# Gated linear attention and a GELU FFN on one core: casts and copies of the second unit on other engines, and a new order

## The chip, the cores and the metric

The kernel runs on one core of a Trainium2 chip. TensorE (PE) multiplies matrices, VectorE (DVE), ScalarE (ACT) and GpSimd (POOL) do the elementwise work, SyncE (SP) issues most of the transfers, and 16 DMA engines carry them. The metric is the time of one execution on the device in microseconds (us), the median of several runs. Lower is better.

## The reference

The first half is a gated linear attention over 4 batches, 8 heads, 768 steps and 48 channels per head, in float32. The second half is an FFN with an exact GELU over the 3072 tokens, with 384 channels and 2048 hidden ones.

```python
f = 1.0 / (1.0 + np.exp(-f_logit))
for t in range(S):
    state = f[:, :, t, :, None] * state + einsum('bhd,bhe->bhde', k[:, :, t], v[:, :, t])
    y[:, :, t] = einsum('bhd,bhde->bhe', q[:, :, t], state)
x = y.transpose(0, 2, 1, 3).reshape(3072, 384)
h = x @ w_in
out = (0.5 * h * (1.0 + erf(h / sqrt(2)))) @ w_out
```

## The kernel before

**Tiles and units.** The 3072 tokens are 24 tiles of 128, numbered n = 0 to 23. Two tiles make a unit u (tiles 2u and 2u+1), the twelve units are loaded and computed one after another, and each ends in one FFN group g = u. For a unit, q, k, v and f_logit are loaded; ACT computes the sigmoid (E, L558) and the log (L, L561) of the gate; a product with a triangular matrix sums the logs (C, L585 to L591); ACT takes the exponentials of the sums (RG and GT, L607 and L613); DVE or POOL multiply keys and queries by these (KP and QP, L640), into the buffers sc. Transposes of sc give kq, on TensorE (Tk and Tq, L876) in units 0 to 3, and by transposing DMAs (KD, L864) from unit 4 on. Score products (A) and masks (AM, L901), products with the state (Y) and within the unit (YI), and the state's own update (S on TensorE, R on DVE, T on POOL) follow; SB casts the state tn to bfloat16 (sb), which the next unit's Y products read. VC casts v to bfloat16 (vb, L647), which S and YI read. YB casts the attention's output (L945), and it is transposed into xT, on TensorE with a copy X behind it (L961, L964), or by DMA from unit 5 on (XD, L949).

**FFN.** A group has eight first products F1.g.u (six matmuls of 128x256, L1165), each followed by one gelu (GE, L1175), and for each of its two tiles four groups F2.n.r of four matmuls (128x384, L1186); O copies the sum and a store (L1200) writes it.

**Banks.** PSUM has eight banks. F1 and F2 use four of them (s_fh), and the attention's products the other four (s_m).

**Queues.** SP's queue issues in program order: whole loads (L513, 384 KB) for the first units, halves of 192 KB (L521) later, the transposing DMAs and the stores. POOL's queue issues the weights: three pieces of w_in (L525, named win0 to win2) and four of w_out (L528). LOADS is the order of all loads in one list; where the list goes over from one engine to the other, `load` lets a POOL load wait until an earlier SP load has landed, and the reverse. ACT needs one function table for exponentials and logs and another for gelus, so each change between them is a table load (L1248).

**What sets the order.** Each operation is added with `P.add(engine, estimated duration, ...)`. The table ORDER lists the operations by number. They are placed, and thereby emitted on each engine, in the order of that list, and an engine never passes an instruction that waits. The estimated durations have a part in the order only through a planner that made the table; with the table given, they place nothing themselves.

Of the kernel before, what the change touches and what calls it, by code (L numbers as in the profile page):

```python
# [10 lines left out]
AF = mybir.ActivationFunctionType  # L11
# [10 lines left out]
TURN = 0.1  # L22
# [53 lines left out]
class Plan:  # L76
# [30 lines left out]
    def run(self):  # L107
# [16 lines left out]
        while ready:  # L124
# [34 lines left out]
            if o.table and o.table != act:  # L159
                act, switched = o.table, t  # L160
                d += TABLE
# [41 lines left out]
HX = [0, 3, 9]  # L203
# [15 lines left out]
SBT = []  # L219
AHEAD = 4.4  # L220
UNITS = 12
WARM = 30.0
LOADS = ['f0', 'f1', 'k0', 'q0', 'v0', 'q1', 'k1', 'i0', 'v1', 'f2', 'q2', 'v2', 'k2', 'i1', 'i2', 'o0', 'o1', 'o3', 'o2', 'f3', 'f4', 'k3', 'q3', 'v4', 'v3', 'q4', 'k4', 'k5', 'f5', 'v5', 'q5', 'f6', 'v6', 'k6', 'q7', 'q6', 'f7', 'k7', 'v7', 'f8', 'k8', 'v8', 'q8', 'u9', 'u10', 'u11']
# [38 lines left out]
def kernel(  # L262
# [105 lines left out]
    P.add("POOL", 1.9, pair_sums, wr=["trip", "negp"], prio=-100)  # L368
    P.add("POOL", 2.6, pair_mask, wr=["maskp"], prio=-85)
# [37 lines left out]
    def load(eng, issue, wr, bufs, dur, name):  # L407
# [22 lines left out]
        if prev is not None and eng != "act" and order[-1][0] != eng:  # L430
            prev.lat = 2.2
# [18 lines left out]
        if 7 <= i and o.lat < 1.8:  # L450
            o.lat = 2.0 if name == "i0" else 1.8 if i < 30 else 1.7
# [23 lines left out]
    for what in LOADS:  # L475
# [12 lines left out]
        elif what[0] in "ucfkqv":  # L488
# [13 lines left out]
            elif x["pair"]:  # L502
                assert what[0] != "c"
                for nm, a in names:
                    if what[0] not in ("u", nm[0]):
                        continue
                    if nm == "fl" and m in SPLIT:
# [7 lines left out]
                        [(nm, 2 * m), (nm, 2 * m + 1)], [x[nm]], 1.5, f"{nm}{m}")  # L515
            else:
                for j in js:
                    for nm, a in names:
                        if what[0] not in ("u", "c", nm[0]):
                            continue  # L520
                        load("sp", lambda x=x, nm=nm, a=a, m=m, j=j: nc.sync.dma_start(  # L521
                            out=half(m, x[nm], j), in_=src(a, 2 * m + j)),
                            [(nm, 2 * m + j)], [x[nm]], 1.05, f"{nm}{m}.{j}")
        elif what[0] == "i" and m < len(WIN):
            load("pool", lambda m=m: nc.gpsimd.dma_start(out=win[m], in_=win_src[:, :, wcol[m]:wcol[m] + WIN[m]]),  # L525
                 [f"win{m}"], [], {512: 2.4, 1024: 4.1}[WIN[m]] + (0.3 if order[-1][0] == "sp" else 0.0), what)
        elif what[0] == "o":
            load("pool", lambda m=m: nc.gpsimd.dma_start(out=wout[m], in_=wo_src[m]), [f"wout{m}"], [], 2.15, what)  # L528


    def decays(u):
# [37 lines left out]
        for j, n in enumerate(ns):  # L569
# [37 lines left out]
            P.add("ACT", 0.40, lambda g=gps[j], rg=rg: nc.scalar.activation(rg.t(), g.t()[:, 0:HD], AF.Exp, scale=-1.0),  # L607
# [5 lines left out]
            P.add("ACT", 0.40, lambda g=gps[j], gtv=gtv: nc.scalar.activation(  # L613
# [668 lines left out]
```

## Time and profile before

| | |
|---|---|
| median of 3 runs | 179.34 us (178.78 to 179.63) |
| span of the profiled execution | 178.1 us |
| busy: PE, ACT, DVE, POOL | 95%, 73%, 53%, 31% of the span |
| granted TensorE clock | 1.00 in each of the stages |
| DMA | 32.61 MB, mean 183 GB/s |

The profiled execution's own time is not listed apart from its span. The time of a run includes what lies around the span, so the 178.1 us are 1.2 us below the median.

A row of the profile reads: start, busy time, engine, line, operation, written tile <- read tiles, shape, count, and in brackets how long the engine sat idle before it and what ended that. Buffer numbers are left out of the names. "PEld" is the loading of weights into TensorE, which overlaps its products. A row can group neighbouring instructions of one line.

### The profile page before, as it was taken

To read this page: it belongs to the slowest core of one execution; us is meant where nothing else is said; L and a number is where in the kernel's file an instruction comes from. 1 tells how busy PE (TensorE), PEld (TensorE's weight loads), DVE (VectorE), ACT (ScalarE), POOL (GpSimd) and SP (SyncE) were. 2 spreads that over 40 slices of the span, in tenths; PEclk is the share of its full clock that TensorE was granted. 3 is DMA by queue.
4 is the path that set the end of the run, shared out by engine and by line. 5 is a ranking of instruction groups with operands and counts; after the bars stand their busy time and mean duration, and the time that the engine had idled before them with its cause. 6 is when DMAs were issued, how large, how long until landed. Compare 5 with 4: busy or idle time off the path is not lost.

```text
span 178.1 us, 4916 instructions
## 1 busy us (share of the span) xinstructions
PE 168.7 (95%) x1996; PEld 131.2 (74%) x1996; DVE 93.7 (53%) x188; ACT 130.0 (73%) x221; POOL 55.2 (31%) x119
## 2 busy tenths in 40 slices
PE   7787889999997999999999999999999999999993
PEld 2345679866787787886688689866797976887972
DVE  5188750067988556338677681246582276560110
ACT  2954399967797999989477597786684789951630
POOL 7267595041126801501052334002222504410000
PEclk9999999999999999999999999999999999999999
DMA  5999999999979898988999999999899975405412
GB/s 140 261 261 214 277 179 195 213 221 256 235 154 227 187 212 188 202 178 169 233 174 248 188 174 204 188 220 156 191 238 179 232 165 81 85 4 112 138 60 88
DMA packets 106997, 32.61 MB, mean 183 GB/s; under 512 B 102112, under 2 KB 106080, under 8 KB 106976
## 3 DMA queue, kind: packets, MB, share of 16 engines
q1 hardware_dynamic: 105056, 29.07, 79.0%
q0 software_dynamic: 1776, 3.15, 10.0%
q8 instruction: 15, 0.25, 0.6%
q10 hardware_dynamic: 144, 0.10, 0.2%
q14 instruction: 6, 0.05, 0.1%
HBM read 25.17 MB, written 4.72 MB: 168 GB/s over the span
## 4 chain that ended last, share of the span: by engine, by line
PE 72%; DMA 14%; SPq 6%; POOL 3%; issue 1%; DVE 1%; ACT 0%; DVEq 0%; POOLq 0%
PE ps L1165 30%; PE ps L1186 29%; DMA vt<-in_v_dram 6%; SPq L513 4%; DMA kt<-in_k_dram 4%; DMA kq<-sc 3%; PE ps L995 2%; PE ps L1031 2%; PE ps L1211 1%; DMA out_dram<-osb 1%; PE ps L585 1%; PE ps L969 1%; SPq L949 1%; SPq L1200 1%; POOL vb L647 1%
## 5 line engine op out<-in xcount | busy, mean ns | idle before, releaser
L1175 ACT ACTIVATE gT<-ps 128x512 bf16<-128x512 f32 x96 | 57.2, 665 | 18.4 <-PE ps L1165 17.6
L1165 PE MATMUL ps<-xT,win 128*128 128x256 bf16 x576 | 69.0, 273 | 0.8 <-DMA win<-in_moe_w_in_dram 0.7
L1186 PE MATMUL ps<-wout,gT 128*128 128x384 bf16 x368 | 67.0, 326 | 0.0
L1165 PEld LDWEIGHTS <-win 128*128 128x128 bf16 x576 | 61.7, 114 | 3.7 <-DMA win<-in_moe_w_in_dram 0.9
L1186 PEld LDWEIGHTS <-gT 128*128 128x128 bf16 x368 | 34.1, 98 | 18.7
L901 DVE TENSOR_TENSOR am<-ps,mask 128x512 bf16<-128x512 f32 x28 | 17.5, 683 | 18.5 <-PE ps L995 18.5
L1248 ACT ACT_TABLE_LOAD x17 | 21.8, 1283 | 0.3
L640 DVE TENSOR_TENSOR sc<-kt,rg 128x384 bf16<-128x384 f32 x19 | 11.5, 606 | 15.8 <-ACT rg L607 11.1
L1191 DVE COPY osb<-ps 128x384 f32<-128x384 f32 x20 | 10.7, 552 | 16.8 <-PE ps L1186 15.7
L927 POOL TENSOR_TENSOR tn<-rr,gl 128x384 f32<-128x384 f32 x12 | 10.7, 889 | 25.1 <-DVE rr L925 19.1
L647 POOL CAST vb<-vt 128x384 bf16<-128x384 f32 x18 | 9.5, 539 | 26.8 <-DMA vt<-in_v_dram 26.6
L901 DVE TENSOR_TENSOR am<-ps,maskp 128x512 bf16<-128x512 f32 x20 | 12.7, 683 | 5.3 <-PE ps L1061 3.8
L945 DVE CAST yb<-ps 128x384 bf16<-128x384 f32 x21 | 11.4, 555 | 7.6 <-PE ps L1031 5.6
L640 DVE TENSOR_TENSOR sc<-qt,gt 128x384 bf16<-128x384 f32 x20 | 13.3, 684 | 3.4 <-ACT gt L613 2.7
L558 ACT ACTIVATE fl<-fl 128x768 f32<-128x768 f32 x12 | 10.1, 842 | 5.0 <-DMA fl<-in_f_logit_dram 5.0
L932 POOL CAST sb<-tn 48x192 bf16<-48x192 f32 x30 | 10.7, 362 | 8.3 <-DVE tn L921 7.1
L613 ACT ACTIVATE gt<-ps 128x384 f32<-128x384 f32 x21 | 10.3, 495 | 3.8 <-PE ps L587 2.9
L607 ACT ACTIVATE rg<-ps 128x384 f32<-128x384 f32 x21 | 10.1, 494 | 3.5 <-PE ps L587 2.9
L640 POOL TENSOR_TENSOR sc<-kt,rg 128x384 bf16<-128x384 f32 x5 | 5.3, 1065 | 22.5 <-ACT rg L607 14.3
L561 ACT ACTIVATE lf<-fl 128x768 bf16<-128x768 f32 x12 | 10.2, 849 | 0.3
L925 DVE TENSOR_TENSOR rr<-ps,tn 128x384 f32<-128x384 f32 x12 | 6.7, 555 | 5.9 <-PE ps L1018 4.8
L1241 PE MATMUL ps<-junk 128*128 128x512 bf16 (+3 forms) x26 | 8.3, 448 | 1.3 <-POOL junk L1233 1.3
(85 smaller groups left out, 145.1 us busy)
## 6 DMA issues: line engine op xcount, KB each, us to landing
out_dram<-osb SPq DMA_DIRECT2D x19, 192.0 KB, 2.8
kt<-in_k_dram SPq DMA_DIRECT2D x14, 192.0 KB, 4.5
fl<-in_f_logit_dram SPq DMA_DIRECT2D x14, 192.0 KB, 3.9
vt<-in_v_dram SPq DMA_DIRECT2D x14, 192.0 KB, 3.9
qt<-in_q_dram SPq DMA_DIRECT2D x14, 192.0 KB, 3.7
fl<-in_f_logit_dram SPq DMA_DIRECT2D x5, 384.0 KB, 4.9
kt<-in_k_dram SPq DMA_DIRECT2D x5, 384.0 KB, 6.2
qt<-in_q_dram SPq DMA_DIRECT2D x5, 384.0 KB, 6.3
```

The source lines that it names most:

```text
L613: P.add("ACT", 0.40, lambda g=gps[j], gtv=gtv: nc.scalar.activation(gtv(), g.t()[:, 0:HD].rearrange("q (p h d) -> q p h d", h=2, d=D), AF. ...
L640: P.add("POOL" if pl else "DVE", 0.80 if pl else 0.475, lambda a=a, y=y, j=j, w=w, pl=pl, b=(gtv if w else rg): (nc.gpsimd if pl else nc.v ...
L647: P.add("ACT" if hv else "POOL", 0.40 if hv else 0.47, lambda y=y, j=j, hv=hv: (nc.scalar.copy if hv else nc.gpsimd.tensor_copy)(y["vb"].t ...
L901: P.add("POOL" if pl else "DVE", 1.15 if pl else 0.61, lambda hh=hh, pl=pl: (nc.gpsimd if pl else nc.vector).tensor_tensor(ams[hh].t(), ap ...
L927: P.add("POOL", 0.83, lambda: nc.gpsimd.tensor_tensor(tn.t(), rr.t(), glb(), ALU.mult), rd=[("rr", n), ("gl", n)], wr=[("tn", n)], bufs=[r ...
L932: P.add("POOL", 0.36, lambda hh=hh: nc.gpsimd.tensor_copy(sb.t()[64 * hh:64 * hh + D, :, D * hh:D * hh + D], tn.t()[64 * hh:64 * hh + D, : ...
L945: P.add("ACT" if help_ else "DVE", 0.40 if help_ else 0.475, lambda: copier(help_)(yb.t()[:, i, :], yp.t()[:, 0:HD]), rd=[("yp", n)], wr=[ ...
L1165: nc.tensor.matmul(hps.t()[:, i * tok:(i + 1) * tok].rearrange("a (s t) -> a s t", s=s), col(fo)[:, kk, :], xT.t()[:, :, kk, :], start=(kk ...
L1175: nc.scalar.activation(to, fr, AF.Gelu)
L1186: nc.tensor.matmul(op.t()[:, 0:d_model], gT.t()[:, fo, s_ * C:(s_ + 1) * C], wout[fo // 4][:, fo % 4, :], start=(fo == 0), stop=(fo == FO ...
L1191: P.add("DVE" if od else "ACT", 0.475 if od else 0.40, lambda op=op, osb=osb, od=od: copier(not od)(osb.t(), op.t()[:, 0:d_model]), rd=[(" ...
L1248: nc.scalar.preload_act_table_set({"exp": "natural_log_exp_and_others", "gelu": "gelu_and_others"}[o.table])
```

## The change

- VCE sends the cast of tile 2's v to ACT (it was on POOL). TE and SBE send the state product T2 and one of SB2's two casts from POOL to DVE. The copy of xT for tile 3 (X3) goes from ACT to DVE, since 3 leaves HX.
- FM puts F1.1.1 and F1.1.3 into banks of the attention's four.
- In LOADS the second piece of w_in (i1) stands ahead of the third unit's keys (k2).
- ORDER is wholly new.
- Many estimated durations and latencies in `P.add` and `load` are changed; with ORDER given they move nothing by themselves.
- The number of table loads goes from 18 to 22 (among them, the exponentials' one at the program's start is now near the end; gelus 1.6 and 4.6 now each stand alone between two more). TensorE's 1996 matmuls are the same.

```diff
-TURN = 0.1
+TURN = 0.092
...
-HX = [0, 3, 9]
+HX = [0, 9]
...
+VCE = {2: 'ACT'}
+FM = [(1, 1), (1, 3)]
+TE = {2: 'DVE'}
+SBE = {(2, 0): 'DVE'}
+SBD = {"POOL": 0.38, "DVE": 0.22, "ACT": 0.27}
...
-LOADS = [..., 'v1', 'f2', 'q2', 'v2', 'k2', 'i1', 'i2', 'o0', 'o1', 'o3', 'o2', 'f3', ...]
+LOADS = [..., 'v1', 'f2', 'q2', 'v2', 'i1', 'k2', 'i2', 'o0', 'o1', 'o3', 'o2', 'f3', ...]
...
-ORDER = [5 6 2 8 18 10 26 30 ...]
+ORDER = [31 7 5 23 11 9 32 2 ...]
...
+    def copy_on(eng):
+        return {"ACT": nc.scalar.copy, "POOL": nc.gpsimd.tensor_copy, "DVE": nc.vector.tensor_copy}[eng]
...
-            hv = u in HVC
-            P.add("ACT" if hv else "POOL", 0.40 if hv else 0.47, lambda y=y, j=j, hv=hv: (nc.scalar.copy if hv else nc.gpsimd.tensor_copy)(
+            hv = VCE.get(n, "ACT" if u in HVC else "POOL")
+            P.add(hv, {"ACT": 0.40, "POOL": 0.47, "DVE": 0.3}[hv], lambda y=y, j=j, hv=hv: copy_on(hv)(
...
-            P.add("POOL", 0.45, lambda: nc.gpsimd.tensor_tensor(small(tn), small(rr), glb(), ALU.mult),
+            e = TE.get(n, "POOL")
+            P.add(e, 0.29 if e == "DVE" else 0.54, lambda e=e: (nc.vector if e == "DVE" else nc.gpsimd).tensor_tensor(small(tn), small(rr), glb(), ALU.mult),
...
-                P.add("POOL", 0.30, lambda hh=hh, r=r: nc.gpsimd.tensor_copy(sb.t()[r, :, D * hh:D * hh + D], small(tn)[r]),
+                e = SBE.get((n, hh), "POOL")
+                P.add(e, SBD[e], lambda hh=hh, r=r, e=e: copy_on(e)(sb.t()[r, :, D * hh:D * hh + D], small(tn)[r]),
...
-            hps = s_fh.new()
+            hps = (s_m if (g, u) in FM else s_fh).new()
```

**First place: POOL around units 1 and 2.** Names carry buffer numbers here (vb2 is a v cast, tn and sb are the state and its bfloat16 form). Before:

```order
L735 TENSOR_TENSOR tn1_142<-rr0_138,gl0_119 128x192
L647 CAST vb2_105<-vt1_86 128x384
L647 CAST vb3_106<-vt1_86 128x384
L738 CAST sb1_149<-tn1_142 48x4x48 x2
L525 DMA win1_71<-in_moe_w_in_dram 128x3x512
L735 TENSOR_TENSOR tn2_143<-rr1_139,gl1_120 128x192
L738 CAST sb2_150<-tn2_143 48x4x48 x2
L525 DMA win2_72<-in_moe_w_in_dram 128x3x512
L735 TENSOR_TENSOR tn3_144<-rr2_140,gl1_120 128x192
L528 DMA wout0_73<-in_moe_w_out_dram 128x1536
```

Now:

```order
L746 TENSOR_TENSOR tn1_142<-rr0_138,gl0_119 128x192
L750 CAST sb1_149<-tn1_142 48x4x48 x2
L654 CAST vb2_105<-vt1_86 128x384
L529 DMA win1_71<-in_moe_w_in_dram 128x3x512
L750 CAST sb2_150<-tn2_143 48x4x48
L529 DMA win2_72<-in_moe_w_in_dram 128x3x512
L532 DMA wout0_73<-in_moe_w_out_dram 128x1536
L532 DMA wout1_74<-in_moe_w_out_dram 128x1536
L532 DMA wout3_76<-in_moe_w_out_dram 128x1536
L532 DMA wout2_75<-in_moe_w_out_dram 128x1536
```

One of the two casts of vt1, the product tn2 and one of sb2's two casts have left POOL, sb1 now stands ahead of the remaining cast, and the five weight loads stand together.

**Second place: POOL around unit 3's casts and unit 4's first key product.** vb7 and vb8 before, vb6 and vb7 now, are the casts of unit 3's v; sc0 is the product of tile 8's keys (KP8). Before:

```order
L735 TENSOR_TENSOR tn4_145<-rr0_138,gl2_121 128x192
L738 CAST sb4_152<-tn4_145 48x4x48 x2
L647 CAST vb7_110<-vt0_85 128x384
L640 TENSOR_TENSOR sc0_95<-kt0_77,rg1_117 128x8x48
L647 CAST vb8_111<-vt0_85 128x384
L932 CAST sb5_153<-tn5_146 48x4x48 x2
```

Now:

```order
L746 TENSOR_TENSOR tn4_145<-rr0_138,gl2_121 128x192
L750 CAST sb4_152<-tn4_145 48x4x48 x2
L654 CAST vb6_109<-vt0_85 128x384
L654 CAST vb7_110<-vt0_85 128x384
L944 CAST sb5_153<-tn5_146 48x4x48 x2
L647 TENSOR_TENSOR sc0_95<-kt0_77,rg0_116 128x8x48
```

Both casts and the state's casts now stand ahead of the key product.

**Third place: SP's queue around unit 5's output and unit 6's keys.** The DMA_TRANSPOSE of xT is unit 5's (XD11), and the two of kq_127 are unit 6's (KD13 and KD12). Before:

```order
L521 DMA vt_88<-in_v_dram 128x8x48 x2
L521 DMA fl_91<-in_f_logit_dram 128x8x48
L1200 DMA out_dram<-osb_161 128x384
L1200 DMA out_dram<-osb_160 128x384
L949 DMA_TRANSPOSE xT_163<-yb_157 128x6x128
L864 DMA_TRANSPOSE kq_127<-sc_99 128x8x128
L864 DMA_TRANSPOSE kq_127<-sc_100 128x8x128
L1200 DMA out_dram<-osb_158 128x384
L521 DMA fl_91<-in_f_logit_dram 128x8x48
L521 DMA kt_77<-in_k_dram 128x8x48 x2
```

Now:

```order
L525 DMA vt_85<-in_v_dram 128x8x48 x2
L525 DMA fl_91<-in_f_logit_dram 128x8x48
L1212 DMA out_dram<-osb_160 128x384
L525 DMA fl_91<-in_f_logit_dram 128x8x48
L525 DMA kt_77<-in_k_dram 128x8x48 x2
L1212 DMA out_dram<-osb_158 128x384
L1212 DMA out_dram<-osb_159 128x384
L961 DMA_TRANSPOSE xT_164<-yb_157 128x6x128
L876 DMA_TRANSPOSE kq_127<-sc_99 128x8x128
L876 DMA_TRANSPOSE kq_127<-sc_100 128x8x128
```

The second half of the gate's load, the two halves of the keys and one store have come ahead of the three transposes.

More of the change, by code (lines that the diff above doesn't have):

```diff
@@ L160, in run @@
                 act, switched = o.table, t
-                d += TABLE
+                t = max(t, free["ACT"] + TABLE)
             o.start, o.end = t, t + d
@@ L367, in pair_mask @@
                                             base=0, pattern=[[-1, 64]], channel_multiplier=1)
[L368 to L369 removed]
+    P.add("POOL", 1.7, pair_sums, wr=["trip", "negp"], prio=-100)
+    P.add("POOL", 2.1, pair_mask, wr=["maskp"], prio=-85)
     for i in range(NQ):
@@ L449, in load @@
             o.fn = lambda o=o: fn(o)
-        if 7 <= i and o.lat < 1.8:
-            o.lat = 2.0 if name == "i0" else 1.8 if i < 30 else 1.7
+        if eng != "act":
+            o.lat = LANDS.get(name, 1.36 if i < 7 else 1.55 if i < 13 else 1.65 if i < 22 else 2.5 if i < 27 else 3.3 if i < 45 else 2.4)
         order.append((eng, o))
@@ L514 @@
                         out=x[nm].t().rearrange("p (h x) -> p h x", h=H), in_=srcp(a, m)),
-                        [(nm, 2 * m), (nm, 2 * m + 1)], [x[nm]], 1.5, f"{nm}{m}")
+                        [(nm, 2 * m), (nm, 2 * m + 1)], [x[nm]], 1.5 if len(order) < 14 else 1.42, f"{nm}{m}")
             else:
@@ L522 @@
                             out=half(m, x[nm], j), in_=src(a, 2 * m + j)),
-                            [(nm, 2 * m + j)], [x[nm]], 1.05, f"{nm}{m}.{j}")
+                            [(nm, 2 * m + j)], [x[nm]], 0.92, f"{nm}{m}.{j}")
         elif what[0] == "i" and m < len(WIN):
             load("pool", lambda m=m: nc.gpsimd.dma_start(out=win[m], in_=win_src[:, :, wcol[m]:wcol[m] + WIN[m]]),
-                 [f"win{m}"], [], {512: 2.4, 1024: 4.1}[WIN[m]] + (0.3 if order[-1][0] == "sp" else 0.0), what)
+                 [f"win{m}"], [], {512: 1.95, 1024: 4.1}[WIN[m]] + (0.35 if order[-1][0] == "sp" else 0.0), what)
         elif what[0] == "o":
-            load("pool", lambda m=m: nc.gpsimd.dma_start(out=wout[m], in_=wo_src[m]), [f"wout{m}"], [], 2.15, what)
+            load("pool", lambda m=m: nc.gpsimd.dma_start(out=wout[m], in_=wo_src[m]), [f"wout{m}"], [], 1.87, what)
+    def copy_on(eng):
+        return {"ACT": nc.scalar.copy, "POOL": nc.gpsimd.tensor_copy, "DVE": nc.vector.tensor_copy}[eng]
     def decays(u):
@@ L639, in decays @@
                 pl = n in (GKP, GQP)[w]
-                P.add("POOL" if pl else "DVE", 0.80 if pl else 0.475, lambda a=a, y=y, j=j, w=w, pl=pl, b=(gtv if w else rg): (nc.gpsimd if pl else nc.vector).tensor_tensor(
+                P.add("POOL" if pl else "DVE", 0.92 if pl else 0.475, lambda a=a, y=y, j=j, w=w, pl=pl, b=(gtv if w else rg): (nc.gpsimd if pl else nc.vector).tensor_tensor(
                     y["sc"].t()[:, w, :, 0:D].rearrange("q (p h) d -> q p h d", h=2),
@@ L900, in mask_scores @@
                 continue
-            P.add("POOL" if pl else "DVE", 1.15 if pl else 0.61, lambda hh=hh, pl=pl: (nc.gpsimd if pl else nc.vector).tensor_tensor(
+            P.add("POOL" if pl else "DVE", 1.15 if pl else 0.605, lambda hh=hh, pl=pl: (nc.gpsimd if pl else nc.vector).tensor_tensor(
                 ams[hh].t(), aps[hh].t().rearrange("p (h t) -> p h t", t=C),
@@ L931, in carry @@
         for hh in range(2):
-            P.add("POOL", 0.36, lambda hh=hh: nc.gpsimd.tensor_copy(
+            P.add("POOL", 0.38, lambda hh=hh: nc.gpsimd.tensor_copy(
                 sb.t()[64 * hh:64 * hh + D, :, D * hh:D * hh + D],
@@ L1065, in attn_pair @@
                 if jk:
-                    P.add("PE", 0.70, lambda: [b[1]() for b in both], mode=1, rd=[("kq", n) for n in ns],
+                    P.add("PE", 0.485, lambda: [b[1]() for b in both], mode=1, rd=[("kq", n) for n in ns],
                           wr=[("ap", u, 0), ("ap", u, 1)], bufs=[kq] + sum([b[2] + b[3] for b in both], []),
@@ L1175, in gelu @@
                 nc.scalar.activation(to, fr, AF.Gelu)
-            P.add("ACT", 0.60 if perm(ns[0]) and ns[0] // 2 not in RST else 0.50, gelu, rd=[("h", g, u)], wr=[("gT", g, u)], bufs=[hps, gT], table="gelu", prio=pr - 1000,
+            P.add("ACT", 0.585 if perm(ns[0]) and ns[0] // 2 not in RST else 0.49, gelu, rd=[("h", g, u)], wr=[("gT", g, u)], bufs=[hps, gT], table="gelu", prio=pr - 1000,
                   name=f"GE{'q' * (s == 4)}{g}.{u}")
```

30 lines of the change are left out of this document (16 added, 14 removed), and 62 rows, old and new, of the table ORDER.

## The prediction

> **What bounds the kernel now.** I read the page first, then its chain of waits and groups, then a table of windows by stage, and then the rows of single engines at the places that the new order touches. The page's head, busy line, slices and groups:
>
> ```profile
> span 178.1 us, 4916 instructions
> PE 168.7 (95%) x1996; PEld 131.2 (74%) x1996; DVE 93.7 (53%) x188; ACT 130.0 (73%) x221; POOL 55.2 (31%) x119
> DMA  5999999999979898988999999999899975405412
> L1175 ACT ACTIVATE gT<-ps 128x512 bf16<-128x512 f32 x96 | 57.2, 665 | 18.4 <-PE ps L1165 17.6
> L1165 PE MATMUL ps<-xT,win 128*128 128x256 bf16 x576 | 69.0, 273 | 0.8 <-DMA win<-in_moe_w_in_dram 0.7
> ```
>
> TensorE is busy for 95% of the span, and of the other engines none reaches 75%. The first FFN product alone is 69.0 of them, and almost nothing in its group's last column is waiting. The change keeps all 1996 matmuls, so it can win only time in which TensorE waits, and lose only by new waits. The windows say where waits are (length, then busy time of PE, PEld, DVE, ACT, POOL, the granted clock, the DMA share, GB/s):
>
> ```profile
> 20.00:24.00 4.00, 3.57 (x90) 2.74 (x89) 2.57 (x7) 2.97 (x3) 3.69 (x9) 1.00 1.15 247
> 24.00:60.00 36.00, 35.05 (x471) 28.15 (x470) 21.71 (x41) 31.05 (x53) 13.70 (x30) 1.00 1.01 210
> 60.00:100.00 40.00, 39.92 (x470) 31.39 (x468) 22.76 (x43) 34.60 (x57) 11.03 (x23) 1.00 1.01 197
> 100.00:140.00 40.00, 40.00 (x412) 32.42 (x410) 20.77 (x38) 28.42 (x55) 9.92 (x16) 1.00 1.00 193
> 140.00:178.10 38.10, 35.00 (x341) 27.92 (x339) 13.61 (x23) 22.27 (x36) 5.76 (x12) 1.00 0.44 102
> ```
>
> After 20 us TensorE is idle for 0.43 + 0.95 + 0.08 + 0.00 + 3.10 us, and the 3.10 is the last evacuation and store behind the last product. So some 1.5 us can be had in the middle, plus junk products put in as filler and waits inside grouped rows. The DMA engines are full (share 1.0 or more in these means) up to 140 us: a transfer moved forward moves another one back. The clock is 1.00 throughout. The first FFN product waits for the first piece of w_in, with the same work ahead of it in both kernels:
>
> ```profile
> 19.35 1.50 PE L1165 MATMUL ps<-xT,win 128*128 128x256 bf16 x12 [0.69 <-DMA win<-in_moe_w_in_dram]
> 20.68 0.54 PE L1241 MATMUL ps<-junk 128*128 128x512 bf16 x2
> 23.59 0.33 PE L975 MATMUL ps<-sb,kq 128*128 128x96 bf16 x4 [0.43 <-POOL sb L738]
> 24.28 0.27 PE L1241 MATMUL ps<-junk 128*128 128x256 bf16 x1
> 54.35 0.52 PE L1093 MATMUL ps<-vb,sc 64*128 64x96 bf16 x16 [0.94 <-POOL vb L647]
> ```
>
> So what happens before 19.35 us is not touched, and the gain lies in the rows behind it.
>
> **The change part by part.** *Second unit's casts and copies.* POOL now makes one of two casts there (ACT has the other), and loses one state product and one state copy to DVE:
>
> ```profile
> 19.64 0.96 POOL L647 CAST vb<-vt 128x384 bf16<-128x384 f32 x2 [2.47 <-DMA vt<-in_v_dram]
> 21.36 0.81 POOL L525 DMA_DIRECT2D win<-in_moe_w_in_dram  x1
> 22.23 0.50 POOL L735 TENSOR_TENSOR tn<-rr,gl 128x192 f32<-128x192 f32 x1
> 22.80 0.74 POOL L738 CAST sb<-tn 48x192 bf16<-48x192 f32 x2
> 20.97 0.84 ACT L558 ACTIVATE fl<-fl 128x768 f32<-128x768 f32 x1 [2.32 <-DMA fl<-in_f_logit_dram]
> L964 DVE COPY xT<-ps 128x384 bf16<-128x384 bf16 x7 | 2.3, 352 | 1.4 <-PE ps L961 1.4
> win<-in_moe_w_in_dram POOLq DMA_DIRECT2D x2, 384.0 KB, 6.5
> ```
>
> Both casts would be there at about 20.15 (19.64 + 0.5), since ACT is idle for 2.32 us before 20.97 and takes its cast for nothing. The state product then follows the two FFN products at 20.68 with no junk ahead of it. The junk row is 0.54 long and overlaps its neighbours by some 0.07, so that is 0.47. The 0.43 at 23.59 goes too: POOL's product and its second copy stand behind a weight issue of 0.81, and on DVE, idle there, they do not. Of the last filler, 0.27 at 24.28, I take 0.2. Start: 0.47 + 0.43 + 0.2 = **1.1 us**, with ends 0.9 and 1.2. The copy of X3 (xT of the fourth tile) that goes from ACT to DVE lies beside FFN products: nothing, and 0.35, its own length in the group below, if that cover went.
>
> *w_in's second piece ahead of the third unit's keys.* Its issue moves from 21.36 to about 20.2. It lands 6.5 us after its issue (the last row above, the median of the two smaller pieces), so at 27.9 in this kernel and at 26.7 in the new one, a little sooner without the keys beside it; the product that needs it comes 1.1 earlier, at about 26.5. I take nothing, with 0.3 as the loss and the same as the gain. The two products in attention banks need no gelu to free a bank; ACT is in step there, so nothing, and one gelu's 0.67 as the gain if it were not.
>
> *Casts ahead of KP8 on POOL.* The 0.94 at 54.35 is a state product that waits for a cast queued behind a key product whose keys came late:
>
> ```profile
> 52.51 1.01 POOL L640 TENSOR_TENSOR sc<-kt,rg 128x384 bf16<-128x384 f32 x1 [3.79 <-DMA kt<-in_k_dram]
> 53.46 0.83 POOL L647 CAST vb<-vt 128x384 bf16<-128x384 f32 x1
> ```
>
> With both casts first it doesn't wait. The next product of that unit needs the masked scores that DVE makes, and no row shows when the last of these would be there without the wait; they are likely next in line. I take **0.2**, with ends 0 and 0.94.
>
> *Table loads.* The program has four more of them: 4 x 1.28 = 5.1 us on ACT, by the second row below. ACT has 18.4 us of idle time before its gelus, and TensorE has second products to do meanwhile; nothing, and at most 1.28, one load, where a bank is awaited. The Trainium skill (ScalarE: Activation LUTs, section "What ACT_TABLE_LOAD costs") adds a drain of about 1380 ns to the 1283 ns, which speaks against the change: the four would be 10.7 us. The rows below disagree, with the next ACTIVATE 0.01 us behind the load.
>
> ```profile
> 121.46 0.86 ACT L558 ACTIVATE fl<-fl 128x768 f32<-128x768 f32 x1
> 127.91 1.28 ACT L1248 ACT_TABLE_LOAD   x1
> 129.20 1.09 ACT L1175 ACTIVATE gT<-ps 128x512 bf16<-128x512 f32 x2
> ```
>
> *SP's queue.* This is the term that speaks against. SP issues in order, and in both kernels the transpose of unit 5's output and the two of unit 6's scaled keys and queries (kq) share that queue with the loads. First SP's rows, then two of the chain of waits and two windows:
>
> ```profile
> 83.06 1.15 SPq L1200 DMA_DIRECT2D out_dram<-osb  x2
> 85.70 2.63 SPq L864 DMA_TRANSPOSE kq<-sc  x2
> 89.25 0.73 SPq L521 DMA_DIRECT2D fl<-in_f_logit_dram  x1
> ```
>
> ```profile
> 87.04 4.66 DMA kq<-sc
> 91.74 0.40 PE ps L995 x8
> 79.00:81.00 2.00, 2.00 (x21) 1.41 (x20) 2.00 (x4) 1.51 (x2) 0.00 (x0) 1.00 0.38 72
> 81.00:92.00 11.00, 10.92 (x121) 7.73 (x118) 7.85 (x16) 8.48 (x19) 1.94 (x3) 1.00 1.12 204
> ```
>
> Unit 6's score product starts at 91.74, as soon as its transpose has landed (87.04 + 4.66 = 91.70), so this queue is already on the path. Now the half load of fl that stood behind the transposes, the two of kt and one store stand ahead of them. By issue times that is 3 x 0.73 + 0.58 (half of the two stores' 1.15) = 2.8 us; by bytes, three halves of 192 KB and a store of 192 KB at 204 GB/s, 0.96 each, 3.9. I take 3.1. Against it stands the start: the stream of loads begins when the weights are in, 1.1 earlier (ends 0 and 1.9). And of the idle DMA time between 79 and 81 us, 2.00 x (1 - 0.38) = 1.24, loads that are ready sooner can fill a part; I take 0.55, between none and all. The transpose then lands at 91.70 + 3.1 - 1.1 - 0.55 = **93.15** (ends 91.4, with 2.8, 1.9 and 1.24, and 95.6, with 3.9 and nothing against it). TensorE would be there at about 91: 91.7, less 1.3 gained so far, plus one group of four F2 matmuls (0.65) that now comes earlier. So it waits, and the product starts at 93.2 in place of 91.74. Of these 1.46 the F2 done earlier gives 0.65 back: **+0.8**. The gain of the start is not added: it is in the wait.
>
> The Trainium skill (DMA: Bandwidth & Descriptors, section "Issuing engines are not separate DMA queues") says that transfers started by different engines run on the same 16 engines and interleave, so issuing weights sooner saves only issue time; by it the stream's start would move by 0 and the transpose would land at 94.25, a further 1.1. The share of 1.0 and above in these windows agrees that the engines are shared.
>
> *The end.* In the last stage 42 F1 matmuls take 4.99 us where 48 took 5.40 earlier, so 4.99 - 42 x 5.40 / 48 = 0.27 is waiting for banks, which the new order, with second products between, can save: **-0.27** (ends 0 and -0.27).
>
> ```profile
> 28.30 5.40 PE L1165 MATMUL ps<-xT,win 128*128 128x256 bf16 x48
> 164.19 4.99 PE L1165 MATMUL ps<-xT,win 128*128 128x256 bf16 x42
> ```
>
> **Sum:** +0.8 - 0.27 = +0.5 on the profiled span of 178.1. The median of the three runs, 179.34, lies 1.2 above that span, so I set the difference on the median: about **179.9 us**.
>
> **The rivals.** *A, the gain stays.* The loads that are placed sooner run sooner, the whole 1.24 us of idle DMA time is filled and the weights' start is worth its 1.9, so the kq transpose lands by 91.7 (91.70 + 2.8 - 1.9 - 1.24 = 91.4) and only the gain is left: 1.1 + 0.2 = 1.3, time 178.0 (177.4 with the longer ends, 178.7 with the shorter). For it: the idle slot at 79 us is there. Against it: DMA shares of 1.0 and more on both sides of it.
>
> *B, held later.* On ACT the sigmoid and log of unit 10's second half (the row at 121.46) now stand ahead of the exponentials of unit 9; if those wait for their load, the gelus that follow and the table load (129.19) come 0 to 1 us later, and F1 products wait for a bank. Then of A's 1.3 there remains 0.1 to 0.3: about 179.1.
>
> *C, slower: unit 2's loads are starved.* POOL issues win1, win2 and all four w_out pieces nearly back to back, ahead of SP's loads of unit 2. A load of v took 10.8 us beside win0, against 6.3 at best, 4.5 more. The rows are the landings of v, the issue of unit 2's keys with the landing time of such loads, and POOL's product with these keys:
>
> ```profile
> DMA to landing us min/median/max: 6.3/8.6/10.8
> 19.36 1.29 SPq L513 DMA_DIRECT2D kt<-in_k_dram  x1
> kt<-in_k_dram SPq DMA_DIRECT2D x3, 384.0 KB, 6.2
> 37.25 1.00 POOL L640 TENSOR_TENSOR sc<-kt,rg 128x384 bf16<-128x384 f32 x1 [8.05 <-ACT rg L607]
> ```
>
> In this kernel the keys land at 19.36 + 6.2 = 25.6. If five weight pieces of 384 KB passed wholly ahead of them, at 204 to 247 GB/s (the slowest and the fastest of the windows above up to 24 us and from 81 on), that is 8.0 to 9.6 us, and with the 4.5 a landing at 38.1 to 39.7. POOL's product then comes 0.9 to 2.5 us later than 37.25, TensorE's transposes behind it too, and the gain of the start is gone: 180.2 to 181.8, in the middle 181.0. It decides from a landing at about 36, where the earlier start would begin to wait. Against it: 11 us of slack, and weights and loads share the engines now, so that a whole standstill of one queue is the extreme.
>
> **How the numbers follow.** The forecast has 0.42, A 0.30, B 0.10, C 0.13, others 0.05. The likeliest time is the forecast's, 179.9, with its own range 179.0 to 181.0. The range, 177.7 to 181.6, takes in most of A and C and the transpose's late end. A change under 0.5% (0.9 us: 178.44 to 180.24) could not be told from none. Faster: A without its short end 0.24, others 0.05: 0.29. Slower: C 0.12, the late end of the forecast (a landing over 93.6, which is 0.4 later) 0.15, others 0.03: 0.30. Same: the rest, 0.41.
>
> **What would show it.** Right: no wait of the product of unit 2's state for vb and none for sb near 21 to 24 us; no wait for vb near 53; and then a TensorE wait of 1.5 us or more for kq or xT between 86 and 94, and landings of these 1 us or more later than 91.7. Wrong: TensorE at 99% through 80 to 95 us with the span under 177 (A), waits for a gelu's bank at 126 to 130 (B), or waits on kt or sc between 30 and 40 us (C). If the transposes of unit 6 land before TensorE comes to them, the step on SP's queue is the one that failed.

## The result

The changed kernel takes 180.67 us in the median of 12 runs (179.37 to 184.38), the kernel before 179.24 us (178.48 to 179.90, 12 runs). The ratio is 1.0078 with a 95% interval of 1.0050 to 1.0106. Run again on another occasion it took 180.02 us against 179.15, a ratio of 1.0051 (1.0023 to 1.0079). So the change makes the kernel slower, by 0.5 to 0.8%, about 0.9 to 1.4 us. The medians are of all runs, while a ratio and its interval are worked out from the single runs without those more than 1.5% above the fastest of their kernel, so a ratio need not be the quotient of the two medians beside it. The forecast was 179.9 us with a range of 177.7 to 181.6.

The profiled execution of the changed kernel has a span of 178.4 us and took 180.19. Its page:

```profile
span 178.4 us, 4918 instructions
PE 169.6 (95%) x1993; PEld 130.9 (73%) x1996; DVE 92.5 (52%) x191; ACT 134.8 (76%) x225; POOL 54.7 (31%) x116
L1187 ACT ACTIVATE gT<-ps 128x512 bf16<-128x512 f32 x96 | 57.7, 666 | 20.0 <-PE ps L1177 19.1
L1177 PE MATMUL ps<-xT,win 128*128 128x256 bf16 x576 | 69.3, 273 | 1.3 <-DMA win<-in_moe_w_in_dram 1.0
L1260 ACT ACT_TABLE_LOAD x21 | 26.9, 1283 | 1.1 <-PEq L1278 0.7
```

Three of the 1996 products are missing from the trace. ACT's busy time grew by 4.8 us: the four more table loads are 5.1, and its other work fell by 0.3. The stages up to 140 us, with the same columns as before:

```profile
20.00:24.00 4.00, 3.86 (x102) 3.11 (x101) 2.34 (x7) 3.09 (x4) 2.55 (x5) 1.00 1.13 229
24.00:60.00 36.00, 35.05 (x458) 27.61 (x456) 20.67 (x42) 33.54 (x55) 13.22 (x25) 1.00 1.10 215
60.00:100.00 40.00, 39.56 (x466) 30.85 (x465) 24.00 (x45) 36.73 (x59) 10.81 (x24) 1.00 1.02 202
100.00:140.00 40.00, 39.92 (x434) 31.65 (x432) 21.98 (x40) 30.50 (x56) 11.66 (x19) 1.00 1.01 201
```

TensorE idles less at the start (0.14 us in place of 0.43), 0.95 us from 24 to 60 us as in the profile before, and 0.44 us from 60 to 100 us, where it idled 0.08. The equal 0.95 misleads: the profile before showed a long execution, and the experiments begin with that. TensorE's rows at the start and near 90 us, where the waits now stand:

```profile
20.52 0.44 PE L1097 MATMUL ps<-vb,sc 64*64 64x48 bf16 x32
22.48 0.33 PE L987 MATMUL ps<-sb,kq 128*128 128x96 bf16 x4
23.61 0.49 PE L973 MATMUL ps<-ident,yb 128*128 128x128 bf16 x6
27.46 2.71 PE L1177 MATMUL ps<-xT,win 128*128 128x256 bf16 x23 [0.68 <-DMA win<-in_moe_w_in_dram]
38.43 0.84 PE L888 MATMUL ps<-ident,sc 128*128 128x128 bf16 x12 [0.27 <-DVE sc L647]
89.83 2.16 PE L1177 MATMUL ps<-xT,win 128*128 128x256 bf16 x18 [0.23 <-DMA xT<-yb]
92.52 0.40 PE L1007 MATMUL ps<-kq 64*128 64x128 bf16 x8 [0.21 <-DMA kq<-sc]
```

The waits for vb and sb are gone at 20.52 and 22.48, and the transposes of yb come at 23.61 in place of 24.57. Then, at 27.46, TensorE waits for win1, and near 90 for xT and kq. On SP's queue the two halves of unit 8's keys are now issued ahead of the transposes, and the last of these, issued at 89.27, landed at 92.47. The last row is from the chain of waits:

```profile
81.91 2.42 SPq L525 DMA_DIRECT2D kt<-in_k_dram  x2
86.08 1.24 SPq L961 DMA_TRANSPOSE xT<-yb  x1
87.44 3.10 SPq L876 DMA_TRANSPOSE kq<-sc  x2
```

```profile
89.27 3.21 DMA kq<-sc
```

That chain names a product of DVE at 89.14 ahead of the transpose. It is unit 7's. Unit 6's four products ended at 84.24, and its transposes stood behind the keys, two stores and xT in SP's queue, which issues in order.

A bracket counts only idle time, and the products ahead of a wait hide part of it. Where I say below that TensorE lost so much *of its lead*, I compare the start of an operation with a walk of the same order in which every operation follows the last one at the pace of its kind. By that walk the wait at 27.46 is 0.95, those at 37 and 38 us 0.48 together, and those at 89.8 and 92.5 are 0.55 and 0.37. The 0.48 stands behind win1 too. In the chain of waits the gelus begin after the products that waited for win1; a table load, the exponentials and DVE's products follow, and the transposes at 38.43 wait for these:

```profile
19.93 7.49 DMA win<-in_moe_w_in_dram
29.00 3.96 ACT gT L1187 x7
34.07 1.28 ACT L1260
35.37 0.90 ACT rg L614 x2
37.09 1.30 DVE sc L647 x2
```

That table load isn't one of the four new ones, since the second profile of the kernel before (below) has it at 34.95.

### The profile page after: what moved, and what is told of

Its sections match the earlier page's. It is cut to its first block, busy times and chain, and to the rows that moved or that the text cites. A ratio compares the mean times of both kernels' runs of the same rounds, so it can differ in the third digit from the quotient of the medians.

```text
span 178.4 us, 4918 instructions
## 1 busy us (share of the span) xinstructions
PE 169.6 (95%) x1993; PEld 130.9 (73%) x1996; DVE 92.5 (52%) x191; ACT 134.8 (76%) x225; POOL 54.7 (31%) x116
## 4 chain that ended last, share of the span: by engine, by line
PE 70%; DMA 15%; ACT 5%; SPq 4%; DVE 2%; issue 2%; POOL 0%; DVEq 0%; POOLq 0%
PE ps L1177 29%; PE ps L1198 27%; DMA vt<-in_v_dram 6%; SPq L517 4%; DMA win<-in_moe_w_in_dram 4%; DMA xT<-yb 3%; ACT gT L1187 3%; PE ps L1007 2%; DMA kq<-sc 2%; PE ps L1223 1%; ACT L1260 1%; PE ps L1043 1%; PE ps L592 1%; PE ps L888 1%; PE ps L1030 1%
## 5 line engine op out<-in xcount | busy, mean ns | idle before, releaser
L1198 PE MATMUL ps<-wout,gT 128*128 128x384 bf16 x368 | 66.2, 326 | 0.0
L647 DVE TENSOR_TENSOR sc<-qt,gt 128x384 bf16<-128x384 f32 x20 | 12.7, 651 | 6.0 <-ACT gt L620 5.7
L1253 PE MATMUL ps<-junk 128*128 128x512 bf16 (+2 forms) x23 | 8.0, 469 | 1.9 <-POOL junk L1245 1.3
```

The costliest lines, as they stand in the source:

```text
L647: P.add("POOL" if pl else "DVE", 0.92 if pl else 0.475, lambda a=a, y=y, j=j, w=w, pl=pl, b=(gtv if w else rg): (nc.gpsimd if pl else nc.v ...
L1198: nc.tensor.matmul(op.t()[:, 0:d_model], gT.t()[:, fo, s_ * C:(s_ + 1) * C], wout[fo // 4][:, fo % 4, :], start=(fo == 0), stop=(fo == FO ...
```

## The experiments

**A second look at both kernels.** Both kernels ran once more, unchanged.

> The kernel before as it is, for a second profile of it. The runs so far show spans around 177.0 for it, while the profile that the prediction was made from had 178.1. Theory 1 (that profile shows one long execution, and its 0.94 us wait for vb is what was long in it): span 176.6 to 177.3, the state product of unit 3 waits under 0.3 us for vb, because unit 4's keys land before POOL comes to them. Rival (the wait is there in each execution, and the extra 1.1 us lies elsewhere): a wait of 0.7 to 1.0 at 54 us.

> The changed kernel as it is, a second time. Its profiled execution was only 0.3 us longer than that of before, its median 1.4 us. Theory 1 (the waits that this profile shows are the whole of it, and vary in size from run to run): again 0.3 to 0.8% slower than before, spans spread over 1 us or more, and in a profile with a longer span the same places wait longer: the F1 product for win1 near 27, the transposes of keys near 38, the F1 product for xT and the scores for kq near 90 to 92. Theory 2 (something outside these places): a longer span with these waits unchanged.

The kernel before gave a span of 176.9 us, not 178.1, and the median span of its runs is 177.0. Unit 4's keys were there sooner, and the state product of unit 3 didn't wait. POOL's and TensorE's rows:

```profile
51.00 1.38 POOL L640 TENSOR_TENSOR sc<-kt,rg 128x384 bf16<-128x384 f32 x1 [2.29 <-DMA kt<-in_k_dram]
53.32 0.51 PE L1093 MATMUL ps<-vb,sc 64*128 64x96 bf16 x16
```

In its chain of waits the scores of unit 6 follow an F2 product. They did not wait for kq, which had landed at 89.56 (issued at 84.78, 4.78 us):

```profile
89.66 0.65 PE ps L1186 x4
90.31 0.55 PE ps L995 x16
```

So the profile that the prediction was made from showed an execution 1.1 us longer than usual, and both its 0.94 us wait for vb and its tight kq were part of that. Theory 1 of the first text held. In this execution TensorE hardly idles in the middle:

```profile
24.00:60.00 36.00, 35.98 (x477) 28.61 (x476) 21.23 (x41) 32.05 (x54) 14.41 (x32) 1.00 1.07 215
60.00:100.00 40.00, 40.00 (x471) 31.49 (x470) 23.71 (x45) 33.58 (x56) 9.92 (x20) 1.00 0.98 201
```

So against the usual execution the changed kernel idles 0.93 us more from 24 to 60 us, at win1 and at the third unit's transposes, and 0.44 more from 60 to 100 us. More of the new idle time lies ahead of 60 us than near 90; against it stands the start, where TensorE idles 0.40 less from 20 to 24 us (0.14 against 0.54).

The changed kernel took 180.02 us, and this time the profile caught a long execution (span 180.3). It waits longer for win1, and in one place that the first profile hardly shows:

```profile
128.95 2.40 PE L1177 MATMUL ps<-xT,win 128*128 128x256 bf16 x18 [0.54 <-DVE osb L1203]
128.34 0.56 DVE L1203 COPY osb<-ps 128x384 f32<-128x384 f32 x1 [2.73 <-PE ps L1177]
```

The wait for win1 costs 1.67 us of lead in that run, and the work at unit 8's F1 products 1.5 us: about 1.0 at these products, which wait for a bank, and the rest at the scores behind them, which wait for DVE as well. The bank is held until DVE has copied an FFN output. The view names a product of TensorE as what DVE waited for, 2.73 us, but that product was long over; the store that frees the buffer landed at 128.22, just ahead of the copy. This was a longer execution than most, and such a wait alone is no proof; the kernel with the lone gelu joined, below, lost 0.8 us of lead at the same place in an ordinary one. So in that execution the added time lies in the same kind of wait, and one of the places was new: theory 1 held for win1, not for the list of places.

**The start alone.** In the kernel before, tile 2's cast, its state product and one of two state copies move as in the change, and the copies of tile 1's state go ahead of the cast. win1 keeps its place in the list of loads. The code, shortened:

```diff
-            hv = u in HVC
+            hv = u in HVC or n == 2
...
-            P.add("POOL", 0.45, lambda: nc.gpsimd.tensor_tensor(small(tn), small(rr), glb(), ALU.mult),
+            P.add("DVE" if n == 2 else "POOL", ..., lambda: (nc.vector if n == 2 else nc.gpsimd).tensor_tensor(small(tn), ...),
```

> The kernel before with the start of the change alone: tile 2's v cast on ACT, its state product and one of two state copies on DVE, the copies of tile 1's state ahead of the cast on POOL; TensorE's order, banks and loads as before. Prediction's step: 0.9 to 1.2 us faster. Theory 1 (win1's landing, 27.4 to 28.0, is next in line, and the F1 product that needs it came at 28.3): the waits between 20.7 and 24.6 shrink by 0.9 to 1.2 us, 0.4 to 0.9 of it returns as a wait for win1, and the median is 0 to 0.5 us (0 to 0.3%) below before.

178.88 us against 179.10, a ratio of 0.9982 (0.9954 to 1.0009); the median span is 177.1 against 177.0. The waits went and came back as waits for the weights:

```profile
20.66 0.44 PE L1085 MATMUL ps<-vb,sc 64*64 64x48 bf16 x32
23.78 0.51 PE L961 MATMUL ps<-ident,yb 128*128 128x128 bf16 x6 [0.27 <-DVE yb L945]
27.86 0.33 PE L1241 MATMUL ps<-junk 128*128 128x384 bf16 x1
28.30 5.43 PE L1165 MATMUL ps<-xT,win 128*128 128x256 bf16 x48
```

The wait for win1 shows as the filler at 27.86 and the gap behind it. The transfer itself, from the chain of waits, was issued at 21.35, as in the kernel before:

```profile
21.35 6.90 DMA win<-in_moe_w_in_dram
```

At 23.78 TensorE is 0.7 us ahead of the second profile of the unchanged kernel (24.45), and at 28.30, the first product with win1 (landed at 28.25), it is where that one is too (28.24). Theory 1 held: the start is worth nothing while win1 comes when it does.

**Letting win1 through.** In the changed kernel the third unit's keys are listed behind win1, but SP issued them at 19.36 and POOL issued win1 at 19.93, so they shared the engines. Two kernels make the keys wait, the first for win1's landing, the second for that of the queries:

```diff
+        if name == "kt2":
+            gate = order[-1][1]     # the second: order[-3][1]
         prev = order[-1][1] if order else None
```

> The changed kernel, but the load of the third unit's keys waits until the second piece of w_in has landed; nothing else. In the changed kernel these keys were issued at 19.36, ahead of win1's issue at 19.93, and shared the engines with it. Theory 1 (win1 is late because it shares): win1 lands 0.7 to 1.5 us earlier than 27.4, the 0.7 us of TensorE waiting there goes, and the keys land near 32, still ahead of 37. But the gain is used up at the transposes of unit 5 and 6 near 90 us, whose landing it does not move: span 0 to 0.4 us shorter. Rival (the weights' rate is what limits win1, whoever shares): landing and wait unchanged. Rival 2 (the gain survives): 0.7 to 0.9 us shorter.

> The changed kernel, but the third unit's keys wait for the landing of its queries (22.3), between the changed kernel (keys issued at 19.36, landed at 28.3, win1 at 27.4 to 28.0) and the one where they waited for win1 (issued at 26.6, landed at 38.9, win1 at 26.6). Theory 1 (POOL's weights are served first, and what SP issues beside them gets what is left): win1 lands at 26.6 to 27.0; the keys land between 30 and 37, so whether TensorE waits at 38 us decides: below 36.5 the kernel is 0 to 0.5 us faster than the changed one, the rest used up near 90. Rival (the keys fall behind all weights as soon as they are issued behind win1): landing near 37 to 38, and 1 to 3 us slower than the changed kernel.

With the first, 183.36 us, 1.0227 of before (1.0192 to 1.0261). Two steps of its chain of waits, then TensorE's row, then two windows:

```profile
20.34 6.24 DMA win<-in_moe_w_in_dram
26.60 12.30 DMA kt<-in_k_dram
```

```profile
40.47 0.61 PE L890 MATMUL ps<-ident,sc 128*128 128x128 bf16 x4 [3.68 <-POOL sc L649]
```

```profile
36.00:41.00 5.00, 1.32 (x10) 0.62 (x7) 2.00 (x3) 2.53 (x5) 1.96 (x2) 0.81 1.04 242
41.00:46.00 5.00, 5.00 (x58) 3.31 (x60) 1.49 (x3) 3.30 (x4) 1.22 (x4) 0.51 1.27 260
```

win1 landed 0.8 us sooner and the wait for it went, but the keys took 12.3 us behind the weights and TensorE waited 3.68 us for them. That is the prediction's rival C, made to happen. None of that run's theories had it; theory 1 put the keys near 32. Behind the wait the granted clock fell to 0.51 for about five microseconds, which costs some 2.4 us more by an estimate from that row (5 x 0.49).

With the second, 181.47 us, 1.0100 (1.0067 to 1.0132). win1 landed at 26.5 and the keys at 34.9, in time, as theory 1 had it, but its time did not follow:

```profile
33.11 3.46 PE L1200 MATMUL ps<-wout,gT 128*128 128x384 bf16 x20 [0.93 <-DMA wout<-in_moe_w_out_dram]
91.81 2.16 PE L1179 MATMUL ps<-xT,win 128*128 128x256 bf16 x18 [1.32 <-DMA xT<-yb]
```

The first second product now waits for w_out, and a later F1 product waits 1.32 for xT. In the three orders tried, win1, the keys and w_out were each late once, and the mean DMA share was 1.04 to 1.18 in each stretch of 5 us from 20 to 35 us. This fits a limit set by the bytes themselves; a kernel with fewer bytes there was not tried.

**The transposes near 90 us.** In the changed kernel unit 8's two key loads go behind the three transposes of SP's queue; then the same with both edits:

```diff
 ORDER: ... XD11 KD13 KD12 placed ahead of kt8.0 kt8.1 (were behind them), nothing else moved
```

> The changed kernel, but on SP's queue the two half loads of unit 8's keys stand behind the transposes of unit 5's output and unit 6's keys again, as in the kernel before; nothing else moves. Theory 1: xT lands near 88.2 in place of 89.8 and the last kq near 90.8 in place of 92.5, the waits of 0.23 and 0.21 in the rows (0.9 us of lag with what the rows hide) go, and the span is 0.6 to 0.9 us shorter: 0.3 to 0.5% faster than the changed kernel. Rival (the stream of transfers is full, so what is put back is late next): unit 8's keys are awaited near 100 us, or the transposes behind them are late, and the span is the same within 0.3 us.

> Both edits of the two runs above in one kernel. Theory 1: the gain of the start (0.7 to 0.9) is no longer used up at the transposes, and theirs (0.6 to 0.9) comes with it: 1.3 to 1.8 us shorter than the changed kernel, so faster than the kernel before by 0 to 0.5 us in the median. Rival (a full stream): no more than either alone, and the time goes into new waits for transfers between 93 and 135 us.

The first took 180.61 us, 1.0077 of before: no gain on the changed kernel. xT landed at 87.1 in place of 89.8, as expected, and the first FFN products did not wait, but a third one did:

```profile
92.05 0.82 PE L1177 MATMUL ps<-xT,win 128*128 128x256 bf16 x6 [0.23 <-DVE osb L1203]
```

```profile
86.66 1.28 ACT L1260
87.95 0.50 ACT gt L620
90.05 1.48 DVE sc L647 x3
91.53 0.48 DVE osb L1203
```

The last four rows are from the chain of waits of the same execution, which was a longer one than this kernel's median (span 179.3 against 178.65), with 1.2 us of waiting for win1 in it. A table load stands ahead of unit 7's exponentials, DVE's products with them ahead of its copies, and the product waits for a bank that such a copy frees. The kernel with both edits took 184.34 us (1.0282): the keys landed at 37.7 and TensorE waited for them as in the first of the last pair. Theory 1 fell for both, in its times: what it said of xT's landing came true.

**The lone gelu.** The table load above is one of the two around gelu 4.6. The next kernel joins this gelu to its group (F1.4.6 and GE4.6 earlier in ORDER, 20 table loads), and another has this with the transposes first.

> The changed kernel, with the gelu 4.6 that stands alone between two table loads joined to the other gelus of its group (its F1 product moved up on TensorE), so two of the four added table loads are gone. In the changed kernel the exponentials of unit 7 begin behind the second of these loads, at 87.03, DVE's products with queries follow them, and DVE's copies of FFN outputs stand behind these. Theory 1 (transfers alone set the places near 90): no change within 0.3 us, since xT and kq land where they did. Rival (ACT's table loads and DVE's queue are next in line behind the transfers): alone also little, but see the run with both.

> The last edit, and with it unit 8's key loads behind the transposes as in the run trfirst. That run by itself gained nothing: its F1 product at 92.05 waited for DVE's copy of an FFN output. Theory 1 (two chains end within half a microsecond of each other near 91 us, one of transfers, one of ACT's table load and DVE's queue; each hides the other): with both loosened the waits between 86 and 93 us go, 0.6 to 1.0 us off the changed kernel's median, which is then within 0.5 us of before. Rival: neither chain matters by itself, the lead is lost to other waits before 135 us, and the median stays where the changed kernel's is.

Alone 180.87 us (1.0109), together 182.35 us (1.0169). The first row is from the gelu's edit alone, where the product still waits for xT (landed at 90.63). The next two are from both edits, where xT landed at 87.53, and the waits near 90 are all gone:

```profile
90.68 2.16 PE L1177 MATMUL ps<-xT,win 128*128 128x256 bf16 x18 [0.49 <-DMA xT<-yb]
```

```profile
90.61 2.13 PE L1177 MATMUL ps<-xT,win 128*128 128x256 bf16 x18
92.67 0.62 PE L1007 MATMUL ps<-kq 64*128 64x128 bf16 x16
104.05 1.47 PE L1177 MATMUL ps<-xT,win 128*128 128x256 bf16 x12 [1.36 <-DMA xT<-yb]
```

The third row is the next wait of that execution. Its chain of waits has the transfer ahead of that product:

```profile
98.43 5.58 DMA xT<-yb
```

Theory 1's mechanism is borne out. In the three profiles TensorE is there at about the same time (90.2 to 90.6, without the wait); with the transposes first alone it waits for DVE's copy, with the gelu joined alone for xT, and with both for neither. Its time is wrong: unit 7's xT, which stands behind the loads that were put back, then came 1.36 us late. Both kernels with the gelu joined also lose about 1.1 us of lead at 83 us, where the exponentials of unit 6 now come behind one more gelu and a state product (L1030) waits for the work on them. That the lead goes to other waits before 135 us is the rival on record.

**Stores sooner.** In the changed kernel the stores of tiles 10 and 11 go ahead of four loads and a transpose on SP's queue (st11 and st10 ahead of qt10.1 in ORDER).

> The changed kernel with two stores (tiles 10 and 11) ahead of two loads of unit 10, a transpose and two loads of unit 11 on SP's queue; in the changed kernel they were issued near 123 to 125 although their data are there long before. In the second run of the changed kernel, 1.9 us longer than the first, DVE's copy of an FFN output waited until one of them had landed (128.2), and TensorE's F1 products of unit 8 for DVE: 1.5 us. Theory 1: these waits go; the changed kernel's median falls by 0.2 to 0.8 us and its runs lie closer together. Rival (the two stores delay the transposes behind them): the F1 products of unit 8 wait for xT, or the scores of unit 9 for kq, and the median stays or rises.

180.37 us, 1.0052 (1.0021 to 1.0084), with runs from 179.02 to 181.58. Its profile shows no wait at unit 8's products, but the first profile of the changed kernel hardly had one either:

```profile
127.21 2.13 PE L1177 MATMUL ps<-xT,win 128*128 128x256 bf16 x18
129.27 0.62 PE L1007 MATMUL ps<-kq 64*128 64x128 bf16 x16
```

Its median lies between the changed kernel's two (180.02 and 180.67), so neither a gain in time nor the removal of that wait is shown. Whether the narrower spread is the stores' doing is open.

**The casts alone.** In the kernel before, VC6 goes ahead of KP8 on POOL; then the same with the first half of unit 8's gate load behind unit 6's transposes.

> The kernel before, with one thing of the change alone: POOL casts unit 3's second v tile ahead of unit 4's first key product, not behind it (the buffer of a later v load changes with it). Theory 1: the 0.9 us wait of the state product for vb near 54 goes, and 0.9 to 1.0 us of it shows in TensorE's lead up to 91 us, where the scores of unit 6 then wait 0.9 to 1.1 for kq in place of 0.24, since its landing at 91.7 does not move: 0 to 0.3 us faster than before. Rival (the lead is kept): 0.7 to 1.0 us, 0.4 to 0.6% faster. Rival 2 (masks are next in line): the wait moves to the product within unit 3, and nothing is left even at 60 us.

> The same, and on SP's queue the first half of unit 8's gate load behind the transposes of unit 6, so that these are issued one load sooner than in the kernel before. Theory 1: kq lands about 0.9 us sooner, at 90.8, and the lead of 0.9 to 1.0 us is kept past 92: 0.6 to 1.0 us, 0.3 to 0.6% faster than before. Rival (a full stream gives nothing for nothing): a wait for a transfer takes the place of it between 92 and 135 us, and the time is that of before within 0.3 us.

179.13 us against 179.12, a ratio of 0.9985 (0.9955 to 1.0016), and 178.97 us, 0.9980 (0.9954 to 1.0007). Neither differs from before by more than its interval. The reason is none of those on record: the wait that the casts remove isn't there in most executions, as the second profile of the kernel before showed. No kernel here beats the kernel before by more than its interval.

## Why the prediction was right, and where it was not

The sign was right, and so was one of the places, the queue of transposes near 90 us. The size was right by luck: a span of 178.6 was worked out for the changed kernel, and its runs have 178.9 and 178.25 in the median, but the span that this was added to was 1.1 too long, and the loss of 0.5 added to it was 0.75 to 1.4 too small. The path differs too. In the forecast the gain of 1.3 lasts to 90 us and is lost there together with 0.8 more. By the walk 0.95 was lost at win1 already, 0.48 near 38 us and 0.92 at xT and kq. Two of the forecast's own signs failed: the waits for xT and kq are 0.44 in the rows and 0.92 by the walk, not 1.5 or more, and kq landed 0.8 after 91.7 in the first profile, not 1 or more (1.45 in the long one). By its steps:

- **The base.** The step "so I set the difference on the median" failed. It took the profiled 178.1 as the usual span, with 1.2 us around it. The usual span is 177.0 and 2.13 us lie around it; the profiled execution was a long one. So the loss in the span was 1.25 to 1.9 us, not 0.5. The changed kernel gives 0.37 of it back outside the span (1.76 in place of 2.13), and 0.9 to 1.4 remain in the medians.
- **The start, 1.1.** The gain is real, 0.96 us at the transposes of yb against the profile before (23.61 against 24.57) and 0.84 against the usual execution (24.45), but "I take nothing, with 0.3 as the loss" for win1 was too small: win1 was issued 1.4 us earlier and landed only 0.55 earlier, at 27.41, where 26.7 was worked out, and the lead lost there is 0.95. The landing time of the row, 6.5 us, was taken for a constant; it became 7.5 with the keys beside it, and 6.24 when these were held back. So the start was worth nothing in the change, and nothing that its interval shows by itself, where win1 was not moved. The transposes near 38 us, which the sum had at nothing, lost another 0.48 behind win1.
- **The stream's start, -1.1.** The first load behind the weights was issued at 35.46 in place of 35.77 (35.97 in the usual execution), so 0.3 to 0.5. With the start alone it was issued at 36.54, though the weights behind win1 were issued about 0.8 earlier, so issuing the same bytes sooner did not make them land sooner. The Trainium skill (DMA: Bandwidth & Descriptors, section "Issuing engines are not separate DMA queues") says that starting DMAs on several engines at once saves only the time of issuing. The trace agrees, and the prediction's sentence on it, with a shift of 0, came nearer than the 1.1 of the sum.
- **SP's queue, 3.1.** kq landed at 92.47. Against the long execution that is 0.8 later, where 1.45 was forecast; against the usual one (89.56) it is 2.9 later, and the idle DMA slot at 79 us, on which 0.55 was put, was of the long execution: its share was 0.38, and 0.59 in the second profile. The term of 3.1 was thus about right, with hardly anything to set against it. That the order of this queue delays the transposes is shown by the run with these first, where xT landed 2.65 us sooner. In the usual execution the scores started at 90.31, in the changed one at 92.52, 2.2 later, with 0.65 of F2 done earlier: 1.55 lost by then, where 0.8 was forecast. Only 0.92 of it was lost at xT and kq. The rest was lost ahead of them, most of it near 38 us.
- **The casts ahead of KP8, 0.2.** Worth nothing: the wait belonged to the long execution.
- **The table loads, nothing.** No wait in the changed kernel's profile has one of the four new ones as its last cause, but the one behind gelu 4.6 is next in line near 91 us, and a wait of 0.23 appears behind it once the transposes come first. As in the prediction's rows, the ACTIVATE behind a load starts 0.01 us after it (86.66 + 1.28, then 87.95), so the drain of about 1380 ns that the Trainium skill adds (ScalarE: Activation LUTs, section "What ACT_TABLE_LOAD costs") isn't seen in these kernels.
- **The end, -0.27.** The wait there is gone in the changed kernel, about as forecast.
- **The rivals.** A failed because the lead gained is lost at win1 already. B's place, the F1 products of unit 8, does wait in a long execution, but for a store's landing, not for unit 10's gate. C did not happen: its sign, a wait on sc between 30 and 40 us, is there (0.27 in the row at 38.43), but the keys had landed at 28.31, long before they were used. The run in which the keys waited for win1 shows that C's margin was smaller than it looked: there a load issued behind POOL's weights took 12.3 us. The slower outcome had 0.30, against 0.41 for no change. A's ends, 178.7 and 177.4, don't follow from the ends of its two terms, which give 178.4 and 177.2.

What remains open is why the runs of the changed kernel differ by 2.9 and 5.0 us where those of before stay within 1.4 to 2.1. Its two profiles differ in the landing of win1, xT and the stores, so it may leave less room between a transfer and its use; this was not shown. No edit to the changed kernel won the loss back, so that the waits named here are the whole of it is argued from the walk, not shown by a run.

## What to carry to other kernels

One profiled execution can be a long one: compare its span with the spans of other runs, or its own time with the median, before a wait in it is counted as a gain. Where the DMA engines are full, ask for each transfer moved forward which one now lands later, and who waits for that; here the lead gained on the compute engines ended at the next transfer. When two chains end close together, as here near 91 us, loosening one may show nothing, and loosening both may show a third.

## What was unexpected

After a wait of 3.68 us in the middle of the kernel, TensorE's granted clock was 0.81 in that stretch and 0.51 in the next five microseconds, then 1.00 again. The time that a run takes around its span is 2.13 us for the kernel before and those with the casts moved, and 1.76 to 1.78 for the changed kernel, the one with the start alone and four others (1.93 in the remaining three). So two kernels of equal span can differ by 0.37 us, a quarter or more of the loss here; no run tells what sets it. The keys' transfer of 384 KB from SP's queue took 6 us when issued at 19.4 in the kernel before, 9.0 at 19.4 in the changed kernel, where win1 was issued 0.6 later, 12.5 at 22.3 and 12.3 at 26.6, the last two among POOL's weight loads.
